# Retention attention ahead of two MLPs on one core: the order of the attention pinned on every engine, more buffers for two tiles, and the weight splits moved within a pair

## The chip, the cores and the metric

One NeuronCore of a Trainium2 chip runs the whole program; the other cores take no part. The metric is the device time of one execution in microseconds, lower is better. The kernel before takes 691.26 us (median of three runs, 689.9 to 692.48).

## The reference

Three layers follow one another, in float32:

```
scores = q @ k.T / sqrt(64) * gamma[h] ** (i - j)  for i >= j, else 0     # 4 batches, 8 heads, 576 tokens, 64 wide
x   = concat over heads of (scores @ v)                                    # 2304 tokens x 512
h   = x @ w_in;  g = h * clip(h + 3, 0, 6) / 6;  x2 = g @ w_out            # 512 -> 2048 -> 512
h2  = x2 @ w2_in; s = h2 * softmax(h2); out = (layernorm(s) * g_ln) @ w2_out   # 512 -> 1024 -> 512
```

The weights arrive as 64-bit words and are turned into float32 pairs on the chip.

## The kernel before, in words

Each matmul operand of the MLPs is held as two float32r parts, a rounded one and the rest, and each product is three matmuls, so 12 matmuls give one 128x512 tile of h.

**Attention (L291 to L422)** works on 16 pairs of heads; four pairs make a batch. The 576 tokens of a pair are four chunks of 128 and a last one of 64. `scores` computes the four diagonal blocks of both heads (PSUM tile s, one buffer) and masks them: head 0 with a multiply on VectorE (st, L337), head 1 with a scaled copy on ScalarE (L341) and a select on POOL (L342). `prep` scales v of a pair on ScalarE (L323). `chunk_states` makes the running state of the pair: matmuls into u (one buffer), a copy on ScalarE (L356) and three steps on VectorE (L358). `last_scores` does the last chunk of 64 (PSUM z, VectorE st4, L369). `values` and `from_states` accumulate the output in PSUM xp (one buffer), and `evac_x` takes it out on VectorE as xa (L395, one buffer), with the factors of tab_sb; xa is split into the two parts xb on ScalarE and POOL (L181, L182) and stored to HBM as xs (L401). The table tab_sb is widened from place_sb by eight POOL copies before the loop (L450, L454).

`attention` yields three times a pair: after `scores`; after `prep` of the next pair, the loads of the pair after that, `chunk_states` and `values` of the pair before; and after `last_scores` and `from_states` of the pair before. The loop at L460 counts these thirds as s, so s = 3 x pair + third.

**Weights.** `Weights.step` loads ahead (L102, two raw buffers of 512 KB, `AHEAD` = 3) and splits one half of a weight: a Prelu on ScalarE (L121), then on VectorE L126, L128, L129, L132 and L135 (every third one's L135 is on POOL), with a ScalarE copy (L127) between. The first MLP stage uses 6 of the 16 feed-forward tiles, twelve halves. The loop at L460 calls `step` from s = 4 on: in the second third of pairs 1 to 4, and in two of three thirds from pair 5 on, until twelve are done in pair 8. From pair 5 on each third also takes two steps of the first MLP, six matmuls (L191 for h, L212 for x2): the six h tiles of the first token block fill pairs 5 to 8, and their x2 tiles, which need all twelve halves, follow in pair 9. An h tile leaves PSUM through ScalarE r (L201), VectorE gf (L202), ScalarE g (L205) and POOL (L206).

**What sets the order.** A scheduler orders each engine's instructions by readiness in its own timeline. `tc.keep_in_program_order` puts an instruction behind the one traced just before it on its engine. Before the change that is used for the attention's matmuls (`mm_a`), the raw weight loads and the Prelu; all other attention work on VectorE, ScalarE, POOL, and the loads and stores on SP's queue, are where the scheduler put them. Each engine then runs its list in order, and a queue waits for its oldest instruction.

After attention the rest of the first MLP (all tokens, then the other ten feed-forward tiles) and the second MLP follow; the change doesn't touch them.

Of the kernel before, what the change touches and what calls it, by code (L numbers as in the profile page):

```python
# [9 lines left out]
F32 = mybir.dt.float32  # L10
# [5 lines left out]
ALU = mybir.AluOpType  # L16
# [42 lines left out]
def retention_hardswish_solu_kernel(ctx, tc, kt, qt, kn, vt, w1, w2i, w2o, gln, decay, place, out):  # L59
# [29 lines left out]
    class Weights:  # L89


        def __init__(self, halves, pin):
            self.pin = pin
            self.todo = list(halves)
            self.raws = []
            self.at = 0

# [14 lines left out]
        def split(self, raw, w, scale=None, done=None):  # L112

            z = p0.tile([128, 512], F32, tag="wz", bufs=2, name="wz")
            t = p0.tile([128, 512], I32, tag="wt", bufs=2, name="wt")
            zi, f = z.bitcast(I32), t.bitcast(F32)

            first = se.activation(  # L121
                out=z, in_=raw[:, :, 1].bitcast(F32), func=ACTF.Prelu, scale=2.0 ** -112, alpha=2.0 ** 32
            )
            if self.pin:
                tc.keep_in_program_order(first)
            ve.tensor_scalar(out=t, in0=zi, scalar1=3, scalar2=None, op0=ALU.logical_shift_left)  # L126
# [13 lines left out]
            if done:  # L140
                done()
# [142 lines left out]
    def at_x(c):  # L284

        return slice(384 + CHUNKS[c].start, 384 + CHUNKS[c].stop)

    def mm_a(*args, **kw):
        tc.keep_in_program_order(nc.tensor.matmul(*args, **kw))  # L289

    def load_pair(pr):  # L291
# [18 lines left out]
        nc.sync.dma_start(out=rn, in_=kn[pr])  # L310
        if pr == 0:
            nc.sync.dma_start(out=place_sb, in_=place)
        raws[pr] = rk, rq, rn.rearrange("p (c d) -> p c d", d=128), rv

    def prep(pr):

        if pr >= NPAIR:
            return
        rv = raws[pr][3]
        v = vs[pr] = pa.tile([128, 2, NV, D], F32, tag="v", bufs=2, name=f"v{pr}")  # L320
        for h in range(2):
            head = 2 * (pr % NP) + h
            se.activation(  # L323
                out=v[:, h].rearrange("p c d -> p (c d)"),
                in_=rv[:, NV * h:NV * h + NV].rearrange("p c d -> p (c d)"),
                func=ACTF.Copy, scale=decay_sb[:, head:head + 1],
            )

    def scores(pr):
# [7 lines left out]
        ve.tensor_tensor(  # L337
            out=st[:, 0].rearrange("p (c q) -> p c q", q=128), in0=sp[:, 0].rearrange("p (c q) -> p c q", q=128),
            in1=mask[:, pr % NP].unsqueeze(1).to_broadcast([128, 4, 128]), op=ALU.mult,
        )  # L340
        se.activation(out=st[:, 1], in_=sp[:, 1], func=ACTF.Copy, scale=GAMMA[2 * (pr % NP) + 1] ** -128)  # L341
        ge.affine_select(  # L342
            out=st[:, 1], in_=st[:, 1], compare_op=ALU.is_ge, fill=0.0,
            base=0, pattern=[[0, 4], [1, 128]], channel_multiplier=-1,
        )

    def chunk_states(pr):
# [7 lines left out]
        at = H + pr % NP  # L355
        se.activation(out=state[:, 0], in_=up[:, 0], func=ACTF.Copy)  # L356
        for c in range(1, 4):
            ve.scalar_tensor_tensor(  # L358
                out=state[:, c], in0=state[:, c - 1], scalar=decay_sb[:, at:at + 1], in1=up[:, c],
                op0=ALU.mult, op1=ALU.add,  # L360
            )

    def last_scores(pr):
# [3 lines left out]
        for h in range(2):  # L367
            mm_a(zp[HEADS[h]], k[HEADS[h], CHUNKS[4]], q[HEADS[h], CHUNKS[4]], start=True, stop=True)
        ve.tensor_tensor(out=st4, in0=zp, in1=mask4[:, pr % NP], op=ALU.mult)  # L369

# [32 lines left out]
    def attention():  # L403

        for pr in range(NPAIR + 1):
            if pr < NPAIR:
                scores(pr)
                yield pr
                prep(pr + 1)
                if pr + 2 >= EARLY:  # L410
                    load_pair(pr + 2)
                chunk_states(pr)
            if pr:
                values(pr - 1)
            yield pr
            if pr < NPAIR:
                last_scores(pr)
            if pr:
# [4 lines left out]


    idle = p0.tile([128, 640], mybir.dt.bfloat16, tag="gf", bufs=2, name="idle")
    ve.memset(idle, 0.0)
# [14 lines left out]
    for h in range(2):  # L441
# [3 lines left out]
        )  # L445
    ve.memset(mhalf, -0.5)
    ve.memset(half, 0.5)
    prep(0)
    for p in range(NP):
        ge.tensor_copy(  # L450
            out=tab_sb[p][:, :512].rearrange("p (c q) -> p c q", q=128),
            in_=place_sb[:, p].unsqueeze(1).to_broadcast([128, 4, 128]),
        )
        ge.tensor_copy(out=tab_sb[p][:, 512:], in_=place_sb[:, p, :64])  # L454
# [277 lines left out]
```

## Time and profile before

| | |
|---|---|
| Runs | 689.9, 691.26, 692.48 us; median 691.26 |
| Profiled execution | 691.26 us, span 689.5 us, mean granted clock 0.995 |
| Busy: PE, VectorE (DVE), ScalarE (ACT), POOL | 669.7, 398.7, 312.0, 259.2 us |
| DMA | 97.95 MB, mean 142 GB/s |

A row of the profile names the engine, the line, the operation, the tile written and read, the count, the busy time and mean, and the idle time of the engine just before, with what ended it. PE's busy time is modelled, so short bursts read longer than they cost. PEld is the weight load of a matmul. SPq is SP's queue, which issues the transfers. DMA share is the mean busy share of the 16 DMA engines.

### The profile page before, as it was taken

To read this page: it belongs to the slowest core of one execution; us is meant where nothing else is said; L and a number is where in the kernel's file an instruction comes from. 1 tells how busy PE (TensorE), PEld (TensorE's weight loads), DVE (VectorE), ACT (ScalarE), POOL (GpSimd) and SP (SyncE) were. 2 spreads that over 40 slices of the span, in tenths; PEclk is the share of its full clock that TensorE was granted. 3 is DMA by queue.
4 is the path that set the end of the run, shared out by engine and by line. 5 is a ranking of instruction groups with operands and counts; after the bars stand their busy time and mean duration, and the time that the engine had idled before them with its cause. 6 is when DMAs were issued, how large, how long until landed. Compare 5 with 4: busy or idle time off the path is not lost.

```text
span 689.5 us, 10522 instructions
## 1 busy us (share of the span) xinstructions
PE 669.7 (97%) x3968; PEld 554.3 (80%) x3968; DVE 398.7 (58%) x625; ACT 312.0 (45%) x532; POOL 259.2 (38%) x253
## 2 busy tenths in 40 slices
PE   6798999999999999999999999999999999999998
PEld 4676677888878988888788888889988888888887
DVE  2789932221781777527756746111478877777780
ACT  3556543524553554426335325213256645545363
POOL 4445631512522242634514404322256435132333
PEclk8999999999999999999999999999999999999999
DMA  8887773013433524154673671017656543323332
GB/s 319 288 296 219 228 230 122 29 47 77 143 132 75 170 92 152 60 183 160 215 269 122 217 242 61 16 46 266 222 123 123 137 77 76 77 62 77 74 79 77
DMA packets 76402, 97.95 MB, mean 142 GB/s; under 512 B 42816, under 2 KB 45120, under 8 KB 75328
## 3 DMA queue, kind: packets, MB, share of 16 engines
q1 hardware_dynamic: 76352, 97.29, 46.8%
q8 instruction: 31, 0.51, 0.3%
q14 instruction: 19, 0.16, 0.1%
HBM read 63.71 MB, written 24.12 MB: 127 GB/s over the span
## 4 chain that ended last, share of the span: by engine, by line
PE 77%; DVE 7%; DMA 6%; issue 4%; POOL 3%; ACT 2%; SPq 1%; DVEq 0%; POOLq 0%; ACTq 0%
PE h L191 20%; PE x L212 17%; PE o L637 14%; PE h L571 14%; PE acc L212 7%; PE xp L289 2%; DMA xs<-xa 2%; POOL g L206 2%; PE s L289 2%; DVE wz L129 1%; DVE wz L132 1%; DMA wraw<-in_w_dram 1%; DMA rq<-in_qt_dram 1%; DVE wt L126 1%; DVE gf L202 1%
## 5 line engine op out<-in xcount | busy, mean ns | idle before, releaser
L206 POOL TENSOR_TENSOR g<-gf,g 128x512 fp32r<-128x512 f32 (+1 forms) x80 | 101.5, 1272 | 200.5 <-ACT g L205 189.0
L212 PE MATMUL x<-g,w 128*128 128x512 f32 x648 | 153.7, 393 | 2.0 <-POOL g L206 1.0
L212 PEld LDWEIGHTS x<-g,w 128*128 128x128 f32 x648 | 120.2, 188 | 29.1 <-POOL g L206 1.7
L191 PE MATMUL h<-xb,w 128*128 128x512 f32 (+1 forms) x600 | 133.9, 360 | 1.6 <-ACT x2p L264 1.6
L191 PEld LDWEIGHTS h<-xb,w 128*128 128x128 f32 x600 | 99.8, 189 | 18.5 <-ACT x2p L264 2.3
L202 DVE SCALAR_TENSOR_TENSOR gf<-r,h 128x512 f32<-128x512 f32 (+1 forms) x80 | 50.4, 630 | 95.8 <-ACT r L201 81.0
L571 PE MATMUL h<-w2i,x2b 128*128 128x512 f32 x432 | 102.0, 389 | 0.0
L637 PE MATMUL o<-w2o,lt 128*128 128x512 f32 (+1 forms) x456 | 101.0, 378 | 0.0
L637 PEld LDWEIGHTS o<-w2o,lt 128*128 128x128 f32 x456 | 82.5, 188 | 16.0
L571 PEld LDWEIGHTS h<-w2i,x2b 128*128 128x128 f32 x432 | 80.6, 188 | 16.3
L191 PE MATMUL h<-xB,w 128*128 128x512 f32 x360 | 82.4, 389 | 0.0
L182 POOL TENSOR_TENSOR lt<-lT,lt 128x512 fp32r<-128x512 f32 x36 | 46.3, 1306 | 93.8 <-ACT lt L181 93.8
L191 PEld LDWEIGHTS h<-xB,w 128*128 128x128 f32 x360 | 67.6, 188 | 14.0
L205 ACT ACTIVATE g<-gf 128x512 fp32r<-128x512 f32 (+1 forms) x80 | 47.0, 588 | 63.8 <-DVE gf L202 63.6
L201 ACT ACTIVATE r<-h,half 128x512 f32<-128x512 f32 (+1 forms) x80 | 50.9, 637 | 49.8 <-PE h L191 49.7
L212 PE MATMUL acc<-g,w 128*128 128x256 f32 (+1 forms) x312 | 62.3, 323 | 0.0
L126 DVE TENSOR_SCALAR wt<-wz 128x512 int32<-128x512 int32 x48 | 33.6, 701 | 45.8 <-ACT wz L121 45.4
L212 PEld LDWEIGHTS acc<-g,w 128*128 128x128 f32 x312 | 50.0, 190 | 6.3
L121 ACT ACTIVATE wz<-wraw 128x512 f32<-128x512 f32 x48 | 31.6, 663 | 31.4 <-DMA wraw<-in_w_dram 19.6
L182 POOL TENSOR_TENSOR xb<-xa,xb 128x512 fp32r<-128x512 f32 (+7 forms) x32 | 26.8, 854 | 35.5 <-ACT xb L181 35.5
L132 DVE TENSOR_TENSOR wz<-wt,wz 128x512 f32<-128x512 f32 x48 | 38.5, 804 | 0.9
L129 DVE SCALAR_TENSOR_TENSOR wz<-wraw,wz 128x512 f32<-128x512 uint32 x48 | 37.0, 773 | 0.8
(79 smaller groups left out, 695.1 us busy)
## 6 DMA issues: line engine op xcount, KB each, us to landing
wraw<-in_w_dram SPq DMA_DIRECT2D x32, 512.0 KB, 4.8
rv<-in_vt_dram SPq DMA_DIRECT2D x16, 320.0 KB, 5.6
x2l<-x2s SPq DMA_DIRECT2D x18, 256.0 KB, 4.5
out_dram<-osb SPq DMA_DIRECT2D x17, 256.0 KB, 2.0
x2s<-x2p SPq DMA_DIRECT2D x16, 256.0 KB, 3.5
wraw<-in_w2i_dram SPq DMA_DIRECT2D x8, 512.0 KB, 4.8
w2is<-wsi SPq DMA_DIRECT2D x8, 512.0 KB, 3.7
wraw<-in_w2o_dram SPq DMA_DIRECT2D x8, 512.0 KB, 4.5
```

The costliest lines, as they stand in the source:

```text
L126: ve.tensor_scalar(out=t, in0=zi, scalar1=3, scalar2=None, op0=ALU.logical_shift_left)
L129: ve.scalar_tensor_tensor(out=z, in0=raw[:, :, 0].bitcast(U32), scalar=2.0 ** -52, in1=z, op0=ALU.mult, op1=ALU.mult)
L132: ve.tensor_tensor(out=z, in0=f, in1=z, op=ALU.add)
L182: ge.tensor_tensor(out=x[:, 1, c], in0=src, in1=f32(x[:, 0, c]), op=ALU.subtract)
L191: nc.tensor.matmul(hp, w1t[ff][:, a, c], xb[t, p][:, b, :n], start=(p == 0 and i == 0), stop=(p == NP - 1 and i == 2),)
L201: se.activation(out=r, in_=hp, func=ACTF.Relu, scale=1.0 / 6.0, bias=half)
L202: ve.scalar_tensor_tensor(out=gf, in0=r, scalar=1.0, in1=hp, op0=ALU.min, op1=ALU.mult)
L205: se.activation(out=g[ff][:, 0], in_=gf, func=ACTF.Copy)
L206: ge.tensor_tensor(out=g[ff][:, 1], in0=gf, in1=f32(g[ff][:, 0]), op=ALU.subtract)
L212: nc.tensor.matmul(acc, w1t[ff][:, a, c], g[:, b], start=(first and i == 0), stop=(last and i == 2))
L571: nc.tensor.matmul(h[:, m], x[:, a, c], w[:, b, m * 512:(m + 1) * 512], start=(d == 0 and j == 0), stop=(d == NP - 1 and j == 2),)
L637: nc.tensor.matmul(op, lt[:, a, ff % 4], w[:, b, c:c + n], start=(ff == 0 and j == 0), stop=(ff == NFF2 - 1 and j == 2),)
```

## The change

`keep` is `keep_in_program_order`, and every attention instruction on VectorE, ScalarE and POOL that evacuates PSUM, scales v or masks gets it; only the split of xa into xb and the stores don't. `last_scores` moves from the last third to right behind `scores`; `prep` of the next pair moves behind the loads and `chunk_states`; the POOL copies of the table move to pairs 0 to 3, one pair's copies each (`widen`), and the load of place_sb from pair 0's loads to pair 1's. xa gets two buffers, the q tile of pairs 3 and on four. A ScalarE copy at the very start brings ScalarE's table load there. `Weights` gets `begin`, which runs the Prelu of the next half early; for these twelve halves the lookahead is 2 in place of 3. In pairs 1 to 4 a half is begun in the second third and split in the last; from pair 5 on split in the first and last thirds and begun in the second. The twelfth is still in pair 8.

```
     class Weights:
...
+        def begin(self):
+            if not self.at == len(self.words) < len(self.todo):
+                return
+            self.load_to(self.at + 1)
             z = p0.tile([128, 512], F32, tag="wz", bufs=2, name="wz")
...
+            self.words.append(z)
...
         def step(self, n=1):
-                self.load_to(self.at + AHEAD)
+                self.load_to(self.at + self.ahead)
+                self.begin()
...
-            rq = pa.tile([128, S], F32, tag="rq", bufs=3, name=f"rq{pr}")
+            rq = pa.tile([128, S], F32, tag="rq", bufs=4, name=f"rq{pr}")
...
-        if pr == 0:
+        if pr == 1:
             nc.sync.dma_start(out=place_sb, in_=place)
...
+    def widen(p):
+        keep(ge.tensor_copy(
+            out=tab_sb[p][:, :512].rearrange("p (c q) -> p c q", q=128),
+            in_=place_sb[:, p].unsqueeze(1).to_broadcast([128, 4, 128]),
+        ))
+        keep(ge.tensor_copy(out=tab_sb[p][:, 512:], in_=place_sb[:, p, :64]))
...
-        xa = pa.tile([128, S], F32, tag="xa", bufs=1, name=f"xa{pr}")
-        ve.tensor_tensor(out=xa, in0=xp[:, 384:960], in1=tab_sb[p], op=ALU.mult)
+        xa = pa.tile([128, S], F32, tag="xa", bufs=2, name=f"xa{pr}")
+        keep(ve.tensor_tensor(out=xa, in0=xp[:, 384:960], in1=tab_sb[p], op=ALU.mult))
...
                 scores(pr)
+                last_scores(pr)
+                if pr < NP:
+                    widen(pr)
                 yield pr
-                prep(pr + 1)
                 if pr + 2 >= EARLY:
                     load_pair(pr + 2)
                 chunk_states(pr)
+                prep(pr + 1)
             if pr:
                 values(pr - 1)
             yield pr
-            if pr < NPAIR:
-                last_scores(pr)
             if pr:
                 from_states(pr - 1)
             yield pr
...
+    ve.memset(half, 0.5)
+    ve.memset(mhalf, -0.5)
+    se.activation(out=gln_sb[:, 0:1], in_=half, func=ACTF.Copy)
     idle = p0.tile([128, 640], mybir.dt.bfloat16, tag="gf", bufs=2, name="idle")
...
-    wq = Weights(w1_halves(range(FA), p0, "w", FA, in_first(FA)), True)
+    wq = Weights(w1_halves(range(FA), p0, "w", FA, in_first(FA)), True, 2)
     for s, pr in enumerate(attention()):
         if s == W_LOAD:
             wq.load_to(2)
-        if s >= W_FROM and (s - W_FROM) % 3 < (1 if pr < A_FROM else 2):
-            wq.step()
+        if s >= W_FROM:
+            wq.load_to(wq.at + 2)
+            if s % 3 == 1:
+                wq.begin()
+            elif s % 3 == 2 or pr >= A_FROM:
+                wq.step()
```

## Rows read from the trace of the kernel before

**Rows 1.** The page: busy time, share of the span and instructions of PE, and the chain that ended last by engine.
```profile
PE 669.7 (97%) x3968; PEld 554.3 (80%) x3968; DVE 398.7 (58%) x625; ACT 312.0 (45%) x532; POOL 259.2 (38%) x253
...
PE 77%; DVE 7%; DMA 6%; issue 4%; POOL 3%; ACT 2%; SPq 1%; DVEq 0%; POOLq 0%; ACTq 0%
```
**Rows 2.** Busy time by stretches: start and end, length, busy time and instructions of each engine, granted TensorE clock, DMA share, GB/s.
```profile
6.50:12.00 5.50, 1.73 (x20) 1.29 (x20) 0.92 (x2) 3.58 (x6) 3.00 (x8) 0.72 1.03 387
12.00:17.50 5.50, 5.34 (x72) 4.92 (x72) 3.20 (x10) 2.21 (x7) 1.27 (x2) 0.66 1.03 389
...
22.40:29.40 7.00, 4.32 (x76) 3.63 (x72) 5.33 (x12) 3.47 (x8) 2.32 (x4) 1.00 0.83 282
29.40:34.90 5.50, 4.37 (x78) 3.63 (x72) 4.58 (x11) 3.47 (x8) 3.62 (x5) 1.00 0.66 199
...
6.50:86.90 80.40, 67.76 (x777) 52.75 (x777) 62.74 (x122) 46.31 (x97) 38.98 (x45) 0.96 0.83 276
...
86.90:201.40 114.50, 114.50 (x840) 91.77 (x839) 45.11 (x79) 48.40 (x90) 38.86 (x39) 1.00 0.37 113
91.40:99.90 8.50, 8.50 (x91) 6.52 (x90) 2.60 (x7) 3.62 (x8) 2.18 (x3) 1.00 0.70 199
```
**Rows 3.** The chain that ended last, in order of time: start, length, what.
```profile
92.61 1.59 PE x L212 x6
...
208.72 16.32 PE x L212 x72
```
**Rows 4.** The timeline of the start: start, length, engine, line, operation, and the idle time before it.
```profile
5.03 1.38 PE L289 MATMUL s<-raw 64*128 64x128 f32 x16
...
6.39 1.28 ACT L323 ACT_TABLE_LOAD   x1 [6.39 <-DMA rv<-in_vt_dram]
...
10.61 1.01 ACT L323 ACTIVATE v<-rv,decay_sb 128x320 f32<-128x320 f32 x2 [1.91 <-DMA rv<-in_vt_dram]
...
11.53 0.57 ACT L341 ACTIVATE st<-s 128x512 f32<-128x512 f32 x1
...
12.16 2.08 PE L289 MATMUL s<-raw 64*128 64x128 f32 x16 [2.00 <-ACT st L341]
```
**Rows 5.** MLP matmuls of PE up to 86.9 us, by groups: count, busy time and mean.
```profile
L191 PE MATMUL h<-xb,w 128*128 128x512 f32 x72 | 20.0, 412 | 0.0
...
L212 PE MATMUL x<-g,w 128*128 128x512 f32 x33 | 9.2, 412 | 1.0 <-DVE gf L202 0.7 <-POOL w L135 0.3
```
**Rows 6.** Who waited for whom up to 87 us: total, times, longest.
```profile
PE xp L289 <- DVE xa L395: 5.7, 5, 2.2
...
PE u L289 <- ACT v L323: 3.2, 4, 1.9
...
DVE xa L395 <- DMA xs<-xa: 1.4, 2, 0.7
```
**Rows 7.** VectorE by groups up to 86.3 us: count, busy time, mean ns, idle before and its releaser.
```profile
L132 DVE TENSOR_TENSOR wz<-wt,wz 128x512 f32<-128x512 f32 x12 | 10.6, 892 | 0.1
L126 DVE TENSOR_SCALAR wt<-wz 128x512 int32<-128x512 int32 x12 | 8.3, 697 | 2.7 <-ACT wz L121 2.7
L358 DVE SCALAR_TENSOR_TENSOR state<-state,decay_sb,u 128x64 f32<-128x64 f32 x30 | 8.2, 275 | 6.2 <-ACT state L356 5.9
...
L337 DVE TENSOR_TENSOR st<-s,mask 128x512 f32<-128x512 f32 x10 | 6.8, 681 | 6.4 <-PE s L289 6.4
L395 DVE TENSOR_TENSOR xa<-xp,tab_sb 128x576 f32<-128x576 f32 x9 | 6.8, 750 | 1.4 <-DMA xs<-xa 1.4
L135 DVE TENSOR_TENSOR w<-wz,w 128x512 fp32r<-128x512 f32 x8 | 6.5, 822 | 0.3
L202 DVE SCALAR_TENSOR_TENSOR gf<-r,h 128x512 f32<-128x512 f32 x6 | 4.1, 677 | 1.3 <-ACT state L356 1.3
L369 DVE TENSOR_TENSOR st<-z,mask 128x64 f32<-128x64 f32 x11 | 2.4, 217 | 3.1 <-PE z L289 3.1
```
**Rows 8.** The timeline at the end of the twelfth split.
```profile
84.94 1.28 POOL L135 TENSOR_TENSOR w<-wz,w 128x512 fp32r<-128x512 f32 x1 [2.47 <-DVE st L369]
...
86.28 0.73 PE L212 MATMUL x<-g,w 128*128 128x512 f32 x2 [0.26 <-POOL w L135]
...
86.94 1.16 PE L289 MATMUL s<-rq,rk 64*128 64x128 f32 x16
```
**Rows 9.** Transfers up to 87 us by line: count, KB each, median us from issue to landing.
```profile
wraw<-in_w_dram SPq DMA_DIRECT2D x12, 512.0 KB, 5.3
...
place_sb<-in_place_dram SPq DMA_DIRECT2D x1, 256.0 KB, 5.1
```
**Rows 10.** POOL by groups up to 86.9 us: the longer copies of the table.
```profile
L450 POOL COPY tab_sb<-place_sb 128x512 f32<-128x512 f32 x4 | 2.5, 616 | 3.9 <-DMA place_sb<-in_place_dram 3.9
```
**Rows 11.** The timeline: the first and the last VectorE step of the first split.
```profile
16.33 0.43 DVE L126 TENSOR_SCALAR wt<-wz 128x512 int32<-128x512 int32 x1
...
18.85 0.69 DVE L135 TENSOR_TENSOR w<-wz,w 128x512 fp32r<-128x512 f32 x1
```
**Rows 12.** What SP's queue waited for up to 90 us: total, times, longest.
```profile
SPq L102 <- DVE wz L129: 20.2, 9, 3.9
SPq L303 <- PE xp L289: 8.8, 5, 5.1
```
**Rows 13.** The step L132 up to 87 us: shortest, median and longest duration in ns.
```profile
L132 DVE TENSOR_TENSOR wz<-wt,wz x12: 675/682/1668, 18.1 to 84.1; 128x512 f32<-128x512 f32 x12
```

More of the change, by code (lines that the diff above doesn't have):

```diff
@@ L89, in retention_hardswish_solu_kernel, with __init__ @@
     class Weights:
-        def __init__(self, halves, pin):
-            self.pin = pin
+        def __init__(self, halves, pin, ahead=AHEAD):
+            self.pin, self.ahead = pin, ahead
             self.todo = list(halves)
             self.raws = []
+            self.words = []
             self.at = 0
@@ L107, in step @@
             for _ in range(min(n, len(self.todo) - self.at)):
-                self.load_to(self.at + AHEAD)
+                self.load_to(self.at + self.ahead)
+                self.begin()
                 self.split(self.raws[self.at], *self.todo[self.at][1:])
                 self.at += 1
-        def split(self, raw, w, scale=None, done=None):
+        def begin(self):
+            if not self.at == len(self.words) < len(self.todo):
+                return
+            self.load_to(self.at + 1)
             z = p0.tile([128, 512], F32, tag="wz", bufs=2, name="wz")
-            t = p0.tile([128, 512], I32, tag="wt", bufs=2, name="wt")
-            zi, f = z.bitcast(I32), t.bitcast(F32)
             first = se.activation(
-                out=z, in_=raw[:, :, 1].bitcast(F32), func=ACTF.Prelu, scale=2.0 ** -112, alpha=2.0 ** 32
+                out=z, in_=self.raws[self.at][:, :, 1].bitcast(F32), func=ACTF.Prelu, scale=2.0 ** -112, alpha=2.0 ** 32
             )
@@ L125, in split @@
                 tc.keep_in_program_order(first)
+            self.words.append(z)
+        def split(self, raw, w, scale=None, done=None):
+            z = self.words[self.at]
+            t = p0.tile([128, 512], I32, tag="wt", bufs=2, name="wt")
+            zi, f = z.bitcast(I32), t.bitcast(F32)
             ve.tensor_scalar(out=t, in0=zi, scalar1=3, scalar2=None, op0=ALU.logical_shift_left)
@@ L286, in at_x @@
         return slice(384 + CHUNKS[c].start, 384 + CHUNKS[c].stop)
+    keep = tc.keep_in_program_order
     def mm_a(*args, **kw):
-        tc.keep_in_program_order(nc.tensor.matmul(*args, **kw))
+        keep(nc.tensor.matmul(*args, **kw))
     def load_pair(pr):
@@ L322, in prep @@
             head = 2 * (pr % NP) + h
-            se.activation(
+            keep(se.activation(
                 out=v[:, h].rearrange("p c d -> p (c d)"),
@@ L326, in prep @@
                 func=ACTF.Copy, scale=decay_sb[:, head:head + 1],
-            )
+            ))
     def scores(pr):
@@ L336, in scores @@
                 mm_a(sp[:, h, CHUNKS[c]], k[HEADS[h], CHUNKS[c]], q[HEADS[h], CHUNKS[c]], start=(c == 0), stop=(c == 3))
-        ve.tensor_tensor(
+        keep(ve.tensor_tensor(
             out=st[:, 0].rearrange("p (c q) -> p c q", q=128), in0=sp[:, 0].rearrange("p (c q) -> p c q", q=128),
             in1=mask[:, pr % NP].unsqueeze(1).to_broadcast([128, 4, 128]), op=ALU.mult,
-        )
-        se.activation(out=st[:, 1], in_=sp[:, 1], func=ACTF.Copy, scale=GAMMA[2 * (pr % NP) + 1] ** -128)
-        ge.affine_select(
+        ))
+        keep(se.activation(out=st[:, 1], in_=sp[:, 1], func=ACTF.Copy, scale=GAMMA[2 * (pr % NP) + 1] ** -128))
+        keep(ge.affine_select(
             out=st[:, 1], in_=st[:, 1], compare_op=ALU.is_ge, fill=0.0,
             base=0, pattern=[[0, 4], [1, 128]], channel_multiplier=-1,
-        )
+        ))
     def chunk_states(pr):
@@ L355, in chunk_states @@
         at = H + pr % NP
-        se.activation(out=state[:, 0], in_=up[:, 0], func=ACTF.Copy)
+        keep(se.activation(out=state[:, 0], in_=up[:, 0], func=ACTF.Copy))
         for c in range(1, 4):
-            ve.scalar_tensor_tensor(
+            keep(ve.scalar_tensor_tensor(
                 out=state[:, c], in0=state[:, c - 1], scalar=decay_sb[:, at:at + 1], in1=up[:, c],
                 op0=ALU.mult, op1=ALU.add,
-            )
+            ))
+    def widen(p):
+        keep(ge.tensor_copy(
+            out=tab_sb[p][:, :512].rearrange("p (c q) -> p c q", q=128),
+            in_=place_sb[:, p].unsqueeze(1).to_broadcast([128, 4, 128]),
+        ))
+        keep(ge.tensor_copy(out=tab_sb[p][:, 512:], in_=place_sb[:, p, :64]))
     def last_scores(pr):
@@ L368, in last_scores @@
             mm_a(zp[HEADS[h]], k[HEADS[h], CHUNKS[4]], q[HEADS[h], CHUNKS[4]], start=True, stop=True)
-        ve.tensor_tensor(out=st4, in0=zp, in1=mask4[:, pr % NP], op=ALU.mult)
+        keep(ve.tensor_tensor(out=st4, in0=zp, in1=mask4[:, pr % NP], op=ALU.mult))
     def values(pr):
@@ L445, in retention_hardswish_solu_kernel @@
         )
-    ve.memset(mhalf, -0.5)
-    ve.memset(half, 0.5)
     prep(0)
[L449 to L454, printed above, removed]
     g_a = lambda ff: (p0, "g", FA)
```

## The prediction

> **What bounds the kernel now.** I read the page first: PE is busy for 669.7 of 689.5 us, and the chain that ended last lies on PE for 77% of the span [rows 1]. So time can be won only where PE stands still or runs below its dense pace. The second view, the busy time by stretches, says where that is [rows 2]. From 86.90 us to 201.40 us PE is busy all the time (114.50 of 114.50). Between 6.50 and 86.90 it is busy for 67.76 of 80.40 us. The edges of the stretches from 12 to 34.9 us are the starts of the scores of pairs 1 to 5 (12, 17.5, 22.4, 29.4, 34.9): a pair took 5.5, 4.9, 7.0 and 5.5 us there. What a pair needs is read from the dense stretch 91.40 to 99.90, which holds one pair and three bursts of six MLP matmuls in 8.50 us. A burst takes 1.59 us on the chain [rows 3], so a pair alone is 8.50 - 3 x 1.59 = 3.73 us. From the first scores at 5.03 [rows 4] to those of pair 10 at 86.94 PE does some nine and a half pairs and 72 + 33 MLP matmuls [rows 5], which densely is 9.5 x 3.73 + 105 x 1.59/6 = 63.3 us, in 81.9. **The most that the change can win here is 18.6 us.** (The trace's idle time is less, since the latency of each short burst counts as busy.) What is won here is kept, since the later work hangs on PE.
>
> The third view is who PE waits for before 87 us [rows 6]: VectorE's xa and ScalarE's v. These are queue orders, not amounts: xa waits on VectorE behind a weight split, or for the store of the xa before it. The fourth view, VectorE by groups [rows 7], shows the amount behind it: VectorE is busy 62.74 of the 80.40 us [rows 2], and the larger part of that is the twelve weight splits (L126 to L135). The last thing that PE waits for before it runs dense is the twelfth split: its last step, on POOL, starts at 84.94 and takes 1.28 us, and the matmuls of L212 that wait for it start at 86.28 [rows 8]. So the question of the whole change is: **when does the twelfth split end?**
>
> **The change part by part.** I time the new order by hand, with durations of the trace.
>
> *Start.* ScalarE's table load begins at 6.39 us, when the first v data are there, and takes 1.28 [rows 4]. Done before, it lies beside the wait for data, and v of pair 0 starts 1.28 us earlier. Two VectorE memsets now go ahead of the warm-up matmuls; the cover is the wait for the first keys until 5.03, and without it they would cost a tenth of a microsecond. The place transfer, 256 KB [rows 9], moves on SP's queue behind all four loads of pair 1, which at 387 GB/s [rows 2] land 0.67 us earlier (its v about 9.9 for 10.61). The eight table copies on POOL (0.62 us the long ones [rows 10]) go two at a time behind the mask steps of pairs 0 to 3. The first two end near 12.2 us, and xa of pair 0 wants them near 14; if that cover went, at most their 0.9 us would fall on xa.
>
> Now v of pair 1 stands on ScalarE ahead of st of pair 0, so st runs at 11.53 and the scores of pair 1 wait for it until 12.16 [rows 4]. With v behind st and state, st of pair 0 can run at about 7.5, and the scores of pair 1 start when PE has done u of pair 0, near 9.1: 3.1 us earlier.
>
> *The pins and the place of the split.* For pairs 1 to 4 the split moves from the middle third of a pair to its end, so xa stands ahead of it. But the next st is pinned behind it, and PE's next scores but one wait for that st. So a VectorE round sets the pace: st 0.68, st4 0.22, state 0.83, xa 0.75 [rows 7], a gap of 0.6 before state (5.9 us over ten pairs, same rows) and the split: one runs from 16.33 to 19.54 [rows 11] with a state step and an st4 among it, so 2.7, and 2.8 with a hand-over. That is 5.9 us, or 5.2 where POOL does the last step. With xa of pair 0 near 14.0, pairs 2 to 5 start at 14.0, 19.0, 24.9 and 30.1, against 17.5, 22.4, 29.4 and 34.9: 4.8 us won at pair 5. The round is no shorter than before's; the win is the start and the xa wait.
>
> *Buffers.* A second xa takes away VectorE's 1.4 us of waiting for the xs store [rows 6]. A fourth q and the earlier last-chunk scores take away SP's 8.8 us of waiting for PE before key loads [rows 12]; the q, v, n and weight loads queued behind them on SP move up. The lookahead of two puts a weight load behind its buffer's split, not ahead of it, which cuts most of SP's 20.2 us at L102 [rows 12]. A weight load needs 5.3 us to land [rows 9] and its split comes a pair later, so I cost its later issue at nothing; if SP were held 3 us longer, the Prelu would show it.
>
> The last-chunk scores cost the same in their new place. Starting a split's Prelu one third earlier takes away VectorE's 2.7 us before L126 [rows 7].
>
> *The end of the twelfth split.* VectorE's 62.74 us include what now comes behind the last split in program order: st, state, xa, two st4 and a gf, 0.68 + 0.83 + 0.75 + 0.44 + 0.68 = 3.4. That leaves 59.3. Gaps that stay, by my timing: 2.9 from st of pair 0 to st of pair 1, 1.2 in pair 1, 0.6 in each of pairs 1 to 4, and 0.5 in each of pairs 5 to 8, where the first split's Prelu waits for ScalarE's st: 8.5 us. So 6.5 + 59.3 + 8.5 = 74.3, and 1.3 for the step on POOL: **75.6 us against 86.2**. PE's own work, from 30.1 with 8.5 us a pair, comes to the same point near 71, so VectorE stays the bound. The bounds: with gaps of 5 us the split ends at 72, with 15 at 82.
>
> *What is given back.* While it waited PE had already done 15 matmuls of the next output block (33 of L212 [rows 5], where a block has 18). If the new schedule doesn't move them up, 15 x 0.227 (16.32 us for 72 [rows 3]) = 3.4 us of PE work come later. I charge half, 1.7: 10.6 - 1.7 = 8.9 us.
>
> The profiled execution took 691.26 us for its span of 689.5, and that is the median of the three runs. The forecast is **682.4 us**.
>
> **The rivals.** *VectorE and POOL get in each other's way.* L132 has a median of 682 ns and a longest of 1668 [rows 13], while POOL is busy 38.98 of the 80.40 us [rows 2]. The same work in a shorter stretch raises POOL's share. If each of the eight splits of pairs 5 to 8 pays one such block, 8 x 0.99 = 7.9 us, where the trace already has some 3.5 (12 x 0.21 at L132 and 8 x 0.13 at L135 [rows 7]), 4.4 us of the win go: 686.8. The Trainium skill, page SBUF — State Buffer, section Who interferes with whom, says that a VectorE instruction with two SBUF inputs contends with a GpSimd instruction that reads SBUF, and that the later one is blocked for the whole of the other; L132 is of that kind, and its 1668 ns agree. For this rival: the program order fixes no distance between the two engines. Against: POOL's amount does not grow.
>
> *The transfers are the limit at the start.* From 6.5 to 17.5 us their share is 1.03 [rows 2]. If pairs 1 to 5 can't start earlier than data allow, the 4.8 us at pair 5 shrink to about 1: 686.2. Against: the share falls to 0.83 and 0.66 just where pairs 3 and 4 lose most.
>
> *Slower: ScalarE's fixed queue.* v of the next pair is pinned behind state, and it waits for its data and for PE's last read of the old v. Behind it on ScalarE stand the Prelu and the next st; behind the Prelu the split, behind the split VectorE's next st, and behind that PE's scores. If that wait adds 2 us to each of pairs 1 to 8, 16 us, the 8.9 are lost and 7 more: 698. It decides from about 1.1 us a pair. For it: u waits for v already, 3.2 us [rows 6]. Against: VectorE is the fuller engine, and SP gets loads out earlier.
>
> *Nothing happens.* Instructions without a pin may still be moved, and the schedule may put the splits where they were: 691.
>
> **How the numbers follow.** A change under 0.5% (3.5 us) can't be told from none here. Forecast 0.62; contention 0.10; transfers 0.08; the slower one 0.10; nothing 0.10. Below 687.8 lie the forecast, the transfers and half of contention: 0.75. Within 0.5% lie the other half and the nothing: 0.15. Slower 0.10. The bounds of the split's end, 72 less nothing given back and 82 with 3.4 given back, give 677 and 690.5; PE filling its waits as well could bring 15 us, 676. The range is 675 to 690: it leaves out the slower case and part of the last.
>
> **What would show it.** Right: scores of pair 1 near 9 us and of pair 5 near 30; no waits of xa for xs, nor of SP for PE before key loads; the twelfth split near 76; PE full from there on. Wrong: the last split after 82, ScalarE idle before v for over 1 us a pair, L132 near 1.6 us in most splits, or new idle time of PE after the dense stretch has begun.

## The result, and the profile after

The changed kernel takes 700.12 us (median of four runs, 699.31 to 701.68) against 690.96 us of the kernel before on the same chip: a ratio of 1.0134, 95% interval 1.0106 to 1.0161. It is slower by 9.2 us where a gain of 8.9 was forecast. The profiled execution took 700.62 us for its span of 698.9.

The first view is the matmuls that PE did up to 100 us, in the kernel before and in the changed one (MLP tiles h and x, and scores s from pair 3 on). The 72 of h in the kernel before stand in [rows 5], and so many are done here too.

```profile
L212 PE MATMUL x<-g,w 128*128 128x512 f32 x54 | 15.2, 413 | 1.0 <-DVE gf L202 0.7 <-POOL w L135 0.3
L289 PE MATMUL s<-rq,rk 64*128 64x128 f32 x146 | 10.8, 286 | 0.3 <-DMA rq<-in_qt_dram 0.3
```

```profile
L201 PE MATMUL h<-xb,w 128*128 128x512 f32 x72 | 21.2, 432 | 0.7 <-DVE gf L212 0.7
L222 PE MATMUL x<-g,w 128*128 128x512 f32 x35 | 10.5, 431 | 2.3 <-POOL w L145 2.3
L301 PE MATMUL s<-rq,rk 64*128 64x128 f32 x128 | 11.1, 323 | 5.0 <-ACT st L353 4.9
```

At 100 us the changed kernel is 19 MLP matmuls and 18 score matmuls (a pair has 16) behind. At the prices of the prediction, 1.59 us for six and 3.73 us for a pair [rows 2, 3], that is 5.0 + 3.7 = 8.8 us of the 9.2: nearly the whole loss has happened by 100 us. Pair 15 is still 9.0 us late, so nothing comes back later.

Where it happened shows in the starts of the scores, read from PE's timeline:

| Pair | 1 | 2 | 3 | 4 | 5 | 6 | 7 | 8 | 9 | 10 | 11 | 15 |
|---|---|---|---|---|---|---|---|---|---|---|---|---|
| before | 12.16 | 17.54 | 22.43 | 29.46 | 34.93 | 44.97 | 53.45 | 62.11 | 73.05 | 86.94 | 91.44 | 141.56 |
| changed | 8.99 | 13.30 | 22.05 | 29.59 | 36.32 | 44.98 | 55.14 | 68.23 | 77.53 | 90.80 | 100.38 | 150.58 |

Pairs 1 and 2 start 3.2 and 4.2 us earlier, and by pair 3 all but 0.4 of that is gone. A pair then takes 7.5 and 6.7 us. At pair 6 PE is level in the two kernels: each has done 18 matmuls of h. VectorE is not: the fifth split's long step is 2.9 us late there (kernel before, then changed).

```profile
43.22 0.68 DVE L132 TENSOR_TENSOR wz<-wt,wz 128x512 f32<-128x512 f32 x1
```

```profile
46.09 0.69 DVE L142 TENSOR_TENSOR wz<-wt,wz 128x512 f32<-128x512 f32 x1
```

So the slow rounds took the gain of the start, and the loss against the kernel before comes behind them. Pair 8 is 6.1 us late with the same 54 matmuls of h done; from 45.0 to 68.2 us VectorE is busy for 21.4 of 23.2 us. Pair 10 is 3.9 us late, and between pairs 10 and 11 another 5.1 are lost.

The busy time by stretches answers to [rows 2] (columns as there). PE is not full after 86.90 us, and in the first of the slow rounds its granted clock was 0.61:

```profile
6.50:86.90 80.40, 66.21 (x753) 52.16 (x752) 65.47 (x117) 43.45 (x91) 38.29 (x42) 0.92 0.81 270
86.90:201.40 114.50, 112.19 (x826) 89.51 (x826) 39.42 (x75) 45.53 (x89) 38.90 (x40) 0.99 0.34 103
22.05:29.60 7.55, 6.63 (x74) 5.82 (x74) 6.05 (x11) 3.58 (x10) 3.56 (x5) 0.61 0.90 301
```

One such round, from the timeline of VectorE, ScalarE and POOL in the changed kernel (start, duration, engine, work, and in brackets the idle time before it):

```profile
20.62 0.68 DVE L349 TENSOR_TENSOR st<-s,mask 128x512 f32<-128x512 f32 x1
21.39 0.60 ACT L353 ACTIVATE st<-s 128x512 f32<-128x512 f32 x1 [3.45 <-DVE st L349]
21.89 0.22 ACT L368 ACTIVATE state<-u 128x64 f32<-128x64 f32 x1
21.99 1.01 ACT L335 ACTIVATE v<-rv,decay_sb 128x320 f32<-128x320 f32 x2
...
22.90 0.67 ACT L120 ACTIVATE wz<-wraw 128x512 f32<-128x512 f32 x1
...
23.60 0.43 DVE L136 TENSOR_SCALAR wt<-wz 128x512 int32<-128x512 int32 x1 [0.55 <-ACT wz L120]
23.94 0.75 DVE L415 TENSOR_TENSOR xa<-xp,tab_sb 128x576 f32<-128x576 f32 x1
...
25.06 0.69 DVE L139 SCALAR_TENSOR_TENSOR wz<-wraw,wz 128x512 f32<-128x512 uint32 x1
...
25.44 2.18 POOL L192 TENSOR_TENSOR xb<-xa,xb 128x512 fp32r<-128x512 f32 x2 [2.01 <-ACT xb L191]
25.79 1.66 DVE L142 TENSOR_TENSOR wz<-wt,wz 128x512 f32<-128x512 f32 x1
...
27.55 0.69 DVE L145 TENSOR_TENSOR w<-wz,w 128x512 fp32r<-128x512 f32 x1
...
28.16 0.68 DVE L349 TENSOR_TENSOR st<-s,mask 128x512 f32<-128x512 f32 x1
```

From one st to the next are 7.54 us. 2.98 of them go by before the split can begin: VectorE's st up to 21.30, and then ScalarE's queue (st, state, two v, Prelu) from 21.39 to 23.57. All of the split but its first step runs behind xa, and its L142 meets POOL's xb of that xa. That first step, L136, stands ahead of xa on VectorE, although the split was to come behind it. In the first round xa waits with it for the first weights:

```profile
16.04 0.43 DVE L136 TENSOR_SCALAR wt<-wz 128x512 int32<-128x512 int32 x1 [3.37 <-ACT wz L120]
16.38 0.75 DVE L415 TENSOR_TENSOR xa<-xp,tab_sb 128x576 f32<-128x576 f32 x1
```

VectorE's groups up to 90 us and PE's wait at the twelfth split, which answer to [rows 7, 8] (the last line of the first view is the kernel before's L129, which those rows leave out; it is the changed kernel's L139):

```profile
L142 DVE TENSOR_TENSOR wz<-wt,wz 128x512 f32<-128x512 f32 x12 | 13.8, 1147 | 0.3
L139 DVE SCALAR_TENSOR_TENSOR wz<-wraw,wz 128x512 f32<-128x512 uint32 x12 | 10.4, 865 | 0.3
L136 DVE TENSOR_SCALAR wt<-wz 128x512 int32<-128x512 int32 x12 | 6.2, 518 | 7.8 <-ACT wz L120 7.8
L129 DVE SCALAR_TENSOR_TENSOR wz<-wraw,wz 128x512 f32<-128x512 uint32 x12 | 8.1, 685 | 0.2
```

```profile
86.15 1.20 PE L222 MATMUL x<-g,w 128*128 128x512 f32 x4
89.65 1.22 PE L222 MATMUL x<-g,w 128*128 128x512 f32 x2 [2.31 <-POOL w L145]
90.80 2.08 PE L301 MATMUL s<-rq,rk 64*128 64x128 f32 x16
```

The twelfth split ends at 89.6 us, not at 75.6 (before: 86.2). VectorE waits 7.8 us for a Prelu (before 2.7). Of its split steps L142 and L139 cost 5.5 us more than before and L136 2.1 less; all twelve splits together take 4.4 us more. Then the scores of pair 10 take 2.08 us, where the same tile took 1.16 in pairs 9 and 11: PE had stood still until 89.65, and its granted clock was 0.51 from 89.6 to 92.9 us.

### The profile page after: what moved, and what is told of

Its sections match the earlier page's. It is cut to its first block, busy times and chain, and to the rows that moved or that the text cites. A ratio compares the mean times of both kernels' runs of the same rounds, so it can differ in the third digit from the quotient of the medians.

```text
span 698.9 us, 10517 instructions
## 1 busy us (share of the span) xinstructions
PE 675.3 (97%) x3968; PEld 557.9 (80%) x3968; DVE 402.2 (58%) x625; ACT 312.4 (45%) x533; POOL 261.9 (37%) x253
## 4 chain that ended last, share of the span: by engine, by line
PE 77%; DVE 10%; DMA 6%; issue 3%; ACT 2%; POOL 2%; SPq 1%; DVEq 0%; ACTq 0%; POOLq 0%
PE h L201 19%; PE x L222 19%; PE o L657 14%; PE h L591 14%; PE acc L222 6%; DMA wraw<-in_w_dram 2%; PE xp L301 2%; DVE wz L139 2%; DVE wz L142 2%; DVE wz L138 1%; DVE wt L136 1%; DVE gf L212 1%; PE s L301 1%; DVE w L145 1%; DMA x2s<-x2p 1%
## 5 line engine op out<-in xcount | busy, mean ns | idle before, releaser
L136 DVE TENSOR_SCALAR wt<-wz 128x512 int32<-128x512 int32 x48 | 31.2, 650 | 56.2 <-ACT wz L120 56.1
L192 POOL TENSOR_TENSOR xb<-xa,xb 128x512 fp32r<-128x512 f32 (+7 forms) x32 | 29.8, 949 | 50.5 <-ACT xb L191 50.5
L142 DVE TENSOR_TENSOR wz<-wt,wz 128x512 f32<-128x512 f32 x48 | 43.1, 898 | 1.0
L139 DVE SCALAR_TENSOR_TENSOR wz<-wraw,wz 128x512 f32<-128x512 uint32 x48 | 37.1, 772 | 0.8
(80 smaller groups left out, 699.2 us busy)
```

The lines of the kernel that those rows point to most:

```text
L139: ve.scalar_tensor_tensor(out=z, in0=raw[:, :, 0].bitcast(U32), scalar=2.0 ** -52, in1=z, op0=ALU.mult, op1=ALU.mult)
L192: ge.tensor_tensor(out=x[:, 1, c], in0=src, in1=f32(x[:, 0, c]), op=ALU.subtract)
```

## The experiments

Ratios are to the kernel before on the same chip, with 95% intervals. The difference of two ratios is known to 0.003 or 0.004, some 2 to 3 us. The first four each take one suspect out of the changed kernel.

### e1_old_weights

The changed kernel with the weight loop and the lookahead of the kernel before.

```
-    wq = Weights(w1_halves(range(FA), p0, "w", FA, in_first(FA)), True, 2)
+    wq = Weights(w1_halves(range(FA), p0, "w", FA, in_first(FA)), True)
...
-        if s >= W_FROM:
-            wq.load_to(wq.at + 2)
-            if s % 3 == 1:
-                wq.begin()
-            elif s % 3 == 2 or pr >= A_FROM:
-                wq.step()
+        if s >= W_FROM and (s - W_FROM) % 3 < (1 if pr < A_FROM else 2):
+            wq.step()
```

> The changed kernel with the weights as before the change (Prelu and split together in the middle third of pairs 1 to 4, lookahead 3); start, buffers, pins and last-chunk scores stay changed. If the new place of the split behind ScalarE's v and beside POOL's xb is the whole loss, the start's win stays: scores of pair 2 near 13.3 us, rounds of pairs 2 to 4 near 5.5 us, L142 near 0.7 us there, 683 to 688 us in all. If something else of the change loses (pins, the moved scores), the time stays above 695.

696.54 us, ratio 1.0079 (1.0058 to 1.0101): some 4 us of the loss are the weight loop's. The rest stays. In its first four splits L142 is back at 0.69 us, but in five of the later ones L139 takes 1.55 to 1.67 us beside work of POOL (a mean of 1117 ns over all twelve, for 865).

### e2_begin_first

The Prelu of pairs 1 to 4 begun one third earlier, ahead of state and v on ScalarE (`wq.begin()` at `s % 3 == 0` for those pairs).

> The Prelu of pairs 1 to 4 is begun in the first third, ahead of state and v on ScalarE. Theory ScalarE chain: VectorE's 7.8 us of waiting for the Prelu fall below 4, the rounds of pairs 2 to 4 go from 7.5 to about 6.3 us, and the time falls by 3 to 5 us, to 695 to 697. Theory POOL collision: L142 keeps its 1.65 us in those pairs and the time stays at 699 to 700.

697.5 us, 1.0091 (1.0061 to 1.0122). Pair 10 starts at 86.86, as before the change, but pair 11 at 96.99: 10.1 us for one pair, where the kernel before took 4.5. L142 is at 0.68 to 0.69 us in the first four splits here too, so this run doesn't separate ScalarE's chain from the collision of the next one.

### e3_xb_zero

POOL's part of xb is set to zero (`ge.memset` in place of the subtraction), so POOL reads nothing there.

> POOL sets the second part of xb to zero instead of subtracting (that part of x is left out), so POOL reads nothing there. Theory POOL collision: L142 falls from a mean of 1.15 to under 0.85 us, L139 with it, and the time by 4 to 6 us, to 694 to 696. Theory ScalarE chain alone: VectorE waits for the Prelu as long as now and the time stays within 1.5 us of 700.

697.58 us, 1.0091 (1.0067 to 1.0115). L142 falls from a mean of 1147 to 816 ns, and the run wins about 3 of the 9 us. That is not the price of the collision alone: POOL's part of xb shrinks besides, from 18.7 to 7.4 us up to 95 us, and L136 now takes 1.07 us beside the `memset`, so that the round from 22.72 to 29.93 is still 7.2 us.

### e4_no_pins

`keep` does nothing, except on PE.

> The changed kernel without the new pins on VectorE, ScalarE and POOL. If the pins make the loss: near 691. If the places of the split, the Prelu and v make it: the order of pairs 1 to 4 stays and the time is 698 to 702.

702.54 us, 1.0164 (1.0147 to 1.0182). In the changed kernel the pins are not the loss; without them pair 1 starts at 11.40 in place of 8.99.

### e5_late_k5, e6_before_late_k5, e7_both

The wait for the twelfth split with nothing to fill it, by itself: the ten groups of x2 matmuls that don't need the twelfth split come first.

```
-        for d in range(NP):
...
-            for k, ff in enumerate(ffs):
...
+        if t == 0:
+            order = [(d, k) for d in range(2) for k in range(last)] + [(0, last), (1, last)] + order[2 * last + 2:]
...
+        for d, k in order:
...
```

> The changed kernel, with one change in the order of PE's MLP work in the first token block alone: of output blocks 0 and 1 the ten matmuls groups that need weights 0 to 4 come first, and the two that need the twelfth split last (in the changed kernel block 0 waits for the twelfth split before block 1 begins). No split, no score and no copy moves. Theory of the lost fill: pair 11's scores start 4 to 6 us earlier against pair 10's (in the changed kernel 9.6 us behind it, in the kernel before 4.5), PE's wait of 2.3 us for POOL's w goes, and the run takes 694 to 696. Rival, VectorE's late split alone sets the end: the twelfth split and the time stay, 699 to 701.

> The kernel before, with the same written order of the first block's second matmuls. There the schedule had already put 15 matmuls of output block 1 ahead of the ones that wait, so the theory of the lost fill expects no gain: 690 to 692. If the order helps the kernel before as much as the changed one, 685 to 687, then the fill does not tell the two kernels apart.

> The changed kernel with the written order of the first block's second matmuls and, besides, the Prelu of each split of pairs 1 to 4 begun two thirds of a pair ahead of the split, so that it stands ahead of v and state on ScalarE. If the loss is ScalarE's chain and the lost fill, each for itself, the two gains add up: 2.6 us (as measured for the Prelu alone) and 4 to 6, so 690 to 694, scores of pair 10 near 87 and of pair 11 near 92. If the one swallows the other, 694 to 697.

The changed kernel gains: 697.87 us, 1.0093 (1.0075 to 1.0111), pairs 10 and 11 at 87.93 and 96.56, no wait for POOL's w. The kernel before does not: 691.09, 0.9997 (0.9984 to 1.0011), since its schedule had that fill already. So the lost fill tells the two apart, but it is 2.8 us (0.0041 of 691), not 4 to 6. With the earlier Prelu besides: 693.73, 1.0025 (1.001 to 1.0039). Together they win 7.5 us (0.0109), no less than 2.8 and the 3.0 of e2 (0.0043) added up, and 1.7 us of the loss are left.

### e8_before_start

Now from the other side: parts of the change put alone on the kernel before. First the next pair's v behind the states (with the early table load and the later place transfer).

```
-                prep(pr + 1)
                 if pr + 2 >= EARLY:
                     load_pair(pr + 2)
                 chunk_states(pr)
+                prep(pr + 1)
```

> The kernel before with three edits of the change and no more: the early table load, the place transfer behind the loads of pair 1, and the next pair's v put behind the states in program order. Weights, pins, buffers and last-chunk scores stay as before, so the splits stay ahead of xa, in the middle of a pair. Theory of the moved split: the start's gain (pair 1 near 9, pair 2 near 14) is kept in part at least, and nothing is lost after it: 686 to 690, twelfth split at 82 to 86. Rival, the start is worth nothing since data and VectorE's amount set the later pairs anyway: 690 to 692. Rival, v behind state is itself the loss: 694 or more.

699.2 us, 1.011 (1.009 to 1.013): the last of the three cases expected. The split is written where it was; but with v ahead of the Prelu on ScalarE the schedule puts xa into it, and the round of 7.5 us with L132 at 1.66 beside POOL's xb (2.19) is there, without the rest of the change:

```profile
25.59 0.43 DVE L126 TENSOR_SCALAR wt<-wz 128x512 int32<-128x512 int32 x1 [0.41 <-ACT wz L121]
25.93 0.75 DVE L395 TENSOR_TENSOR xa<-xp,tab_sb 128x576 f32<-128x576 f32 x1
...
27.43 2.19 POOL L182 TENSOR_TENSOR xb<-xa,xb 128x512 fp32r<-128x512 f32 x2 [2.73 <-ACT xb L181]
27.78 1.66 DVE L132 TENSOR_TENSOR wz<-wt,wz 128x512 f32<-128x512 f32 x1
```

### e9_before_buffers

```
-tag="xa", bufs=1 ... tag="rq", bufs=3
+tag="xa", bufs=2 ... tag="rq", bufs=4
```

with the table load and the place transfer.

> The kernel before with the two xa buffers, the four q buffers, the early table load and the place transfer behind pair 1's loads; v, pins, weights and last-chunk scores as before. On ScalarE v of the next pair stays behind the split's Prelu. Theory that v ahead of the Prelu is the loss: nothing is lost here, and VectorE's wait for the xs store before xa (1.4 us in the kernel before) goes: 687 to 691. Rival, the buffers or the table load cost something themselves: 693 or more.

691.23 us, 0.9995 (0.9982 to 1.0008). These parts cost nothing and bring nothing; so e8's loss is put down to v's move, the one part that e9 doesn't share with it.

### e10_v_behind_prelu, e10b_v_behind_prelu_k5, e11_after_old_prep

v's place in the changed kernel: behind the Prelu (without and with the x2 order of above), or where it was before.

```
                 chunk_states(pr)
-                prep(pr + 1)
...
             yield pr
+            if pr < NPAIR:
+                prep(pr + 1)
```

> The changed kernel with one thing moved: the copies of the next pair's v are put behind the split's Prelu (after the values of the pair before, not after the states). On ScalarE the order becomes st, state, Prelu, w, v, and the schedule then puts xa behind the split again, as in the kernel before. Theory that v ahead of the Prelu is the loss: rounds of pairs 2 to 5 fall from 7 or 7.5 us to 5.5 to 6, L142 beside them to 0.68 us, scores of pair 1 stay near 9, twelfth split done by 82 to 85, and the time 684 to 689. Rival, the place of the weight loads and the pins lose the time as well: 694 or more.

> As the kernel with v behind the Prelu, and with the second matmuls of the first block in the order in which the twelfth split's weight comes last. If fill is lost in that kernel too, this wins 1.5 to 3 us more (as it did in the changed kernel), 682 to 687; if its schedule already fills PE, nothing.

> The changed kernel with the next pair's v put back ahead of the states, where the kernel before has it in program order; but pinned there, so that ScalarE runs st, v, state, Prelu. v is still ahead of the Prelu, and the schedule still puts the split behind xa. Theory that v ahead of the Prelu is the loss, whichever side of state it stands: 697 to 702, rounds above 7 us, L142 at 1.65 us in the first splits. Rival, v behind the states is the loss by itself: 688 to 692.

699.23, 698.48 and 697.9 us (1.0117, 1.0097 and 1.0098; 1.0094 to 1.0139, 1.0076 to 1.0118, 1.0077 to 1.0118). For e11 the theory held. In e10b the x2 order wins nothing clear over e10 (the intervals overlap). For e10 it fell as a sole cause: rounds are short (28.51 to 34.28, 5.8 us) and L142 is 0.69 in them, yet nothing is won. What ScalarE waits for up to 90 us points to why:

```profile
ACT wz L120 <- DMA wraw<-in_w_dram: 9.2, 4, 3.6
```

The weights now come too late; in the changed kernel the same wait was 0.8 us. The longer round had hidden it. So another part must lose by itself.

### e12_before_weights, e13_before_pins, e14_before_last_scores, e15_v_prelu_old_weights

The weight loop, the pins and the last-chunk scores, each alone on the kernel before; and the changed kernel with v behind the Prelu and the old weight loop together (the edits of e10 and e1).

> The kernel before with the weight loop of the change and no more: a lookahead of two, the Prelu begun one third ahead, the splits of pairs 1 to 4 written in the last third of a pair. The schedule leaves st, state, Prelu, w, v on ScalarE and the split ahead of xa, as in the kernel before; only the loads are issued later and the splits of pairs 5 to 8 stand in other thirds. Theory that each part breaks the kernel before's period by itself, this one by late loads: ScalarE waits for wraw at the sixth split as in the kernel with v behind the Prelu (3.6 us there), 694 to 698. Rival, only v's move and the pins lose: 690 to 692.

> The kernel before with the pins of the change and no more (st, state, st4, v and xa in program order). v, which stands ahead of the states there, now comes ahead of state and the Prelu on ScalarE; the split still stands ahead of xa. Theory that v ahead of the Prelu or of state costs about 1 us a pair while ScalarE's chain is the round: 694 to 699. Rival, the pins alone cost nothing and the split's place behind xa was the loss: 690 to 692.

> The kernel before with the last chunk's scores moved to the first third of a pair and no more. st4 now stands ahead of state on VectorE, and the schedule puts xa ahead of the split's last step. No theory so far gives this a loss: 689 to 692. If it loses over 2 us, the period of the kernel before depends on st4's place too.

> The changed kernel without two of its parts: v of the next pair behind the Prelu, and the weight loop of the kernel before (lookahead of three, split in the middle third). Pins, buffers, table load, last-chunk scores and the start's order stay. If v's place and the weight loop are the two losses: 688 to 692. If pins or last-chunk scores lose as well: 694 to 698.

| Part alone on the kernel before | us | ratio |
|---|---|---|
| v behind the states (e8) | 699.2 | 1.011 (1.009 to 1.013) |
| weight loop (e12) | 699.13 | 1.0107 (1.0089 to 1.0124) |
| pins (e13) | 697.88 | 1.01 (1.0079 to 1.012) |
| last-chunk scores (e14) | 693.33 | 1.0027 (1.0016 to 1.0038) |
| buffers, table load, place (e9) | 691.23 | 0.9995 (0.9982 to 1.0008) |
| **whole change** | 700.12 | 1.0134 (1.0106 to 1.0161) |
| whole change, v behind the Prelu and old weight loop (e15) | 692.28 | 1.0006 (0.9994 to 1.0018) |

Three parts lose 6 to 8 us each, alone, and together no more than 9. With two of them taken back nothing measurable is lost, though the pins stay: in that order they do no harm that shows. In e12 ScalarE stands at the sixth and the eighth Prelu; its waits for the weights are 8.4 us up to 90 us, against 0.5 in the kernel before. The sixth half's load goes out at 39.38 there and at 36.85 in the kernel before (ScalarE's wait in e12, SP's issue in e12, ScalarE in e12, SP's issue before). The loop holds the lookahead, the early Prelu and the splits' new thirds together; no run took the lookahead alone.

```profile
ACT wz L120 <- DMA wraw<-in_w_dram: 8.4, 3, 4.1
```

```profile
39.38 0.44 SPq L103 DMA_DIRECT2D wraw<-in_w_dram  x1
```

```profile
41.28 0.21 ACT L366 ACTIVATE state<-u 128x64 f32<-128x64 f32 x1
45.55 0.66 ACT L120 ACTIVATE wz<-wraw 128x512 f32<-128x512 f32 x1 [4.07 <-DMA wraw<-in_w_dram]
```

```profile
36.85 0.33 SPq L102 DMA_DIRECT2D wraw<-in_w_dram  x1
```

In e13 st and v are pinned ahead of state, and v waits there for PE's last read of the old v. State waits behind both, and VectorE for state: 16.0 us, against 6.1 in the kernel before (its wait in total, times, longest, up to 90 us; then one such place in the timeline, where PE had done u at 35.3):

```profile
DVE state L360 <- ACT state L358: 16.0, 6, 4.3
```

```profile
34.58 0.69 PE L291 MATMUL u<-v,rn 128*64 128x64 f32 x16
...
36.93 0.58 ACT L343 ACTIVATE st<-s 128x512 f32<-128x512 f32 x1
...
37.84 1.01 ACT L325 ACTIVATE v<-rv,decay_sb 128x320 f32<-128x320 f32 x2 [0.33 <-PE xp L291]
...
38.76 0.20 ACT L358 ACTIVATE state<-u 128x64 f32<-128x64 f32 x1
38.86 0.66 ACT L121 ACTIVATE wz<-wraw 128x512 f32<-128x512 f32 x1
```

The chain of waits from 6.5 to 90 us is led by something else in each: by VectorE's split steps in the changed kernel, by the weight loads in e12, and by the xs store in the kernel before (the view cuts the lines short).

```profile
by line: DVE wz L139 11.3%; issue 10.9%; DVE wz L142 9.2%; DMA wraw<-in_w_dram 7.7%; DVE wz L138 6.8%; DMA raw<-in_qt_dram 6.3%; DVE w L145 6.3%; DMA rn<-in_kn_dram 5.5%; DMA rk<-in_kt_dram 5.2%; DVE wt L136 5.1%; DVE xa L415 4.7%; DVE st L
```

```profile
by line: DMA wraw<-in_w_dram 21.5%; DMA rv<-in_vt_dram 7.3%; issue 6.6%; DVE xa L405 6.0%; PE xp L299 5.5%; DMA rn<-in_kn_dram 5.3%; DVE wz L142 5.3%; SPq L411 4.8%; DVE wz L139 4.6%; PE s L299 4.5%; DVE wt L136 4.2%; DVE wz L138 3.9%; PE x
```

```profile
by line: DMA xs<-xa 13.7%; DMA rq<-in_qt_dram 8.5%; PE h L191 7.6%; DMA rv<-in_vt_dram 7.2%; DVE wz L132 6.6%; PE s L289 6.5%; issue 6.1%; DVE wz L129 5.4%; DVE xa L395 4.4%; DVE wt L126 4.1%; DVE state L358 3.8%; PE xp L289 3.7%; DVE w L13
```

### e16_first_split_late, e17_split_late_old_st4

e15 with its first split one third later (`s == W_FROM + 1` in place of `W_FROM`), and that with `last_scores` back in the last third.

> The changed kernel with v of the next pair behind the Prelu and the weight loop of the kernel before (692.3 us so far), and its first split written one third later, behind xa of pair 0. In the kernel without this ScalarE waits 3.6 us for the first weights at 15.2 us, and the split, xa of pair 0 and the scores of pair 3 wait with it (13.1 to 23.6 us). Theory that the start's gain is stopped there: pair 3 near 20 to 22, pair 5 near 33, and 688 to 691. Rival, the second split then runs into the first, and VectorE's amount sets pair 4 anyway: 691 to 693.

> As the kernel with the first split one third later, and the last chunk's scores back in the third in which the kernel before has them. The last-chunk scores' move alone cost the kernel before 1.8 us (693.3 against 691.5); if that adds up, 1 to 2 us less than the kernel with the first split late; if their place matters only beside the old order of v, the same.

692.16 us, 1.0004 (0.9988 to 1.002), and 694.14, 1.0022 (1.0004 to 1.004). In e16 pairs 1 to 3 start at 9.41, 13.71 and 21.14, but pairs 4 and 5 at 29.93 and 34.82, as before the change: the rival. The last-chunk scores' old place wins nothing here (the intervals of the two kernels overlap). No kernel that was run beats the kernel before.

## Why the prediction was wrong

**The start.** Right: pair 1 at 8.99 (9.1), pair 2 at 13.30 (14.0). That it would be kept was wrong. The first Prelu runs at 15.61 us in the kernel before and no earlier than 15.35 in the changed one and 15.27 in e10, where ScalarE waits 0.8 and 3.6 us for its weights; with the first split begins the slow round, whatever the start has won. xa of pair 0, forecast near 14.0, ran at 16.38, since the split's first step stands ahead of it and waited 3.4 us for that Prelu. So the first round, from pair 2 to pair 3, took 8.75 us where the forecast had 5.0 (14.0 to 19.0, less than either of the rounds that it worked out): the largest single miss up to pair 5. The wait for the weights is the rival of the transfers, in a place that I had not named: the weights' and not the pairs' data. e16 moves the wait but keeps none of the gain at pair 4.

**The round of 5.9 us** is the step that failed, with the weight loads below. It was 7.54 from pair 3 to pair 4, and 6.73 for 5.2 in the next. The sum had VectorE's work and a gap of 0.6 between st and state; the 2.98 us from st to the split are set by ScalarE, 0.65 more than the 2.33 (0.68 + 0.22 + 0.6 + 0.83) that I had put there, because v (1.0 us) stands between state and the Prelu. And split and xa took 4.56 for 3.55, since L142 takes 1.66. 5.88 + 0.65 + 1.01 = 7.54. The earlier Prelu was to take away VectorE's 2.7 us ahead of the split; with v in front of it they became 7.8.

**The weight loads "at nothing".** Wrong as a term: the weight loop alone costs the kernel before 7.4 us (e12). That the loads do this is read from ScalarE's 8.4 us of waiting for them, and not shown by a run that moves them alone. "Its split comes a pair later" holds up to pair 4; from pair 5 on there are two splits a pair, and the sixth load let its Prelu start 6.2 us after the issue (39.38 to 45.55), 4.1 of which ScalarE stood. The text named the sign to look for, the Prelu. In the changed kernel itself the sign is small (0.8 us), since the longer round hides it: with the short rounds of e10 it is 9.2. Taking the loop out of the changed kernel still wins some 4 us (e1). SP's wait at the weight loads fell from 20.2 us [rows 12] to 17.6 only.

**Buffers.** The waits went as forecast (key loads 8.8 to 0.3 us at SP, xa for xs to nothing), and they were worth nothing (e9).

**Last-chunk scores "cost the same".** They lost 1.8 us on the kernel before (e14); putting them back in e16's order won nothing (e17).

**The twelfth split** ended at 89.6 and not at 75.6. Up to the end of its L142 at 87.86 VectorE was busy for 66.4 us and idle for 14.9, where the sum had 59.3 and 8.5. The splits are 4.4 us of the first difference; st, st4 and a gf, 1.6 us, ran ahead of that step, which the sum had put behind it.

**Given back.** I charged half of 3.4 us. The schedule moved none of the next block's matmuls up, and the order that does wins 2.8 (e5), and the slow scores of pair 10 add 0.9.

**The rivals.** "VectorE and POOL get in each other's way" came true in another place than it named. In the eight splits of pairs 5 to 8 L142 took 7.1 us, less than the 7.9 of the kernel before, and only L139 there cost 2 us more; in the four of pairs 1 to 4 L142 took 0.97 to 0.99 us too long each time. Some 3 us went with it in e3, which does not isolate it, so that its 4.4 are near is luck. L142 at 1.66 is 0.98 of waiting and 0.68 of work, beside an xb of 2.18 for 1.57 us. The Trainium skill, page SBUF — State Buffer, section Who interferes with whom, has the later one of the two blocked for the whole of the other; both numbers agree with that. What I had against it, that POOL's amount does not grow, is true of its work and beside the point: up to the twelfth split it runs 44 instructions in both kernels, and is busy for 38.3 us before and 41.0 now, the blocked time included. The place of the split around xa makes them meet each time in pairs 1 to 4. "ScalarE's fixed queue", given 0.10 and 698 us, named the right queue, with v's own 1.0 us in front of the Prelu (e8). The wait of v that it priced at 2 us a pair did not come: up to 90 us v waited in the changed kernel for PE once, 1.8 us at pair 2, and for its data twice at the start. So its 698 us lie near 700.12 partly by luck. Where v is pinned ahead of state, a wait for PE is there (e13). My argument against it, that VectorE is the fuller engine, is a share of busy time; the chain goes through ScalarE between two of VectorE's steps.

What stays open: why e16's and e9's earlier pairs end in the same time. e9's pair 5 starts at 33.64 for 34.93, and pair 13 at 106.26 for 108.45 with 72 matmuls of h and 72 of x2 done in both, yet the medians agree (691.23 and 691.24), and even the profiled execution, e9's fastest, ended only 1.2 us ahead (690.04 and 691.26). So the prediction's "what is won here is kept" is not borne out there. No run isolated the step between pair 3 and pair 4, or the later ones that give e9's gain back; and none took the lookahead, or VectorE's order of L136 and xa, by itself.

## What to carry to other kernels

A queue that is not full can still set the pace: write out one round across all engines, with every instruction that a queue runs between two steps of the full engine, before moving anything in program order. Put each part of a change alone on the kernel before as well as taking it out of the new one: where two waits of like length cover each other, taking one out can show nothing (e10). And a load's slack is counted to the nearest of its uses in the stage where they come thickest.

## What the runs showed of the hardware

A collision of two engines can be locked to the schedule: with xa right behind the split's first step, the 0.68 us step of VectorE took 1.65 to 1.67 us in each of the first four splits of the changed kernel, while POOL's xb, which works on that xa, took 2.17 to 2.20. In the kernel before the same four ran at 0.68, and xb at 1.55 to 1.57.

After some of its waits PE ran at the lower of its two clock levels, 1.2 and 2.4 GHz. It stood for 1.8 us up to 17.18; from 19.00 to 27.50 its granted clock was 0.50, and the 16 score matmuls at 22.05 took 2.08 us. It stood for 2.3 us up to 89.65; from 89.6 to 92.9 the clock was 0.51, and the scores at 90.80 took 2.08. But behind a wait of 1.9 us the scores at 36.32 took 1.16, like those of the other pairs, and the clock was 1.00 from 36.3 to 40.0.
